# One pool of PSUM banks, a first tile in four units, and small decay groups in a fused scan and two-product kernel

## The chip, the cores and the metric

The kernel runs on one core of a Trainium2 chip. The metric is the time of one execution on the device in microseconds (us), the median of several runs. The core has five engines with queues of their own: TensorE (PE; its weight loads are PEld), VectorE (DVE), ScalarE (ACT), GpSimd (POOL) and SyncE (SP), which here issues all transfers.

## The reference

The first half is a gated linear recurrence over 768 steps, for 4 batches of 8 heads of 48 elements. The second is two matrix products with a function between them, on 3072 tokens of 384 elements.

```python
f = 1 / (1 + exp(-f_logit))                       # gate per step, head and key element
state = f[t, :, None] * state + k[t] (outer) v[t] # 48 x 48 per batch and head
y[t] = q[t] @ state
x = y as (4*768 tokens, 8*48)
h = x @ w_in                                      # 384 -> 2048
out = (h * cos(h)) @ w_out                        # 2048 -> 384, float32
```

## The kernel before

**Attention.** The 768 steps of each batch are cut into six chunks of 128 steps, 24 chunks in all. Four loads bring a chunk (`chunk_load`, line 254: f, k, q, v, each 192 KB). `decay_group` (lines 259 to 296) takes three chunks at a time: exponential and logarithm of the gates on ScalarE (lines 267, 270), a cumulative sum over the steps on TensorE with a triangular matrix (line 280), and two exponentials of it, b and bi (line 290). `attend` (lines 298 to 435) scales q and k with them on GpSimd (qtd and ktd, lines 301 and 304), copies v among zeros (vz, line 307), transposes q and k on TensorE (line 318), copies the transposes out (qdt and kz, lines 332 and 334), forms the scores (pa, line 349), masks them (am, line 354), updates the state (ps, st, sz, lines 369 to 388) and sums the output (py, lines 416 and 420) into the tile xT of 512 tokens (lines 432 and 434).

**The two products.** `moe` (lines 438 to 473) works on a tile of 512 tokens, six tiles in all. For each of 16 blocks of 128 hidden features it makes three matmuls into one bank (ph, line 445), a sine on ScalarE (cos(h) as sin(h + pi/2), line 448) and a product on VectorE (gT, line 451). Then for each 128 tokens 16 matmuls form the result (po, line 459), which is copied (line 467) and stored (line 472).

**The order.** Nothing is left to a scheduler at run time. The class `Plan` takes each operation with the engines that may do it and a cost in ns for each, plans them one by one, and the kernel issues them in the order of planned start times. `Plan.run` (lines 77 to 145) chooses, among the operations whose inputs have been planned, the one with the smallest key: planned start, then the priority value (smaller first). An operation that would change ScalarE's function table has 1300 added to the start in its key (lines 109 to 111). The exponential and logarithm share one table (E), the sine has another (S). When the first E operation of a decay group is placed, ScalarE takes no operation with a table from outside the group until all of the group's are placed (the lock, lines 107 and 125). Attention's priority is its chunk's number, that of the products 1000 plus the tile's number (line 493).

**Buffers.** Each kind of tile has its own slots, and a slot is held from the first planned writer to the last planned user. The eight PSUM banks are split: three for ph, one for po, two for pa, two for everything else of attention (lines 217 to 220). Weights are loaded through two staging tiles each for w_in and w_out and cast by VectorE (line 242); the loads are planned behind chunks 1, 2 and 3. Tiles that must be zero outside the written parts are filled at the start, vz, kz and sz on GpSimd (lines 204 to 209).

Of the kernel before, what the change touches and what calls it, by code (L numbers as in the profile page):

```python
# [15 lines left out]
class Slots:  # L16


    def __init__(self, aps):
        self.aps = aps  # L20
        self.free_at = [0.0] * len(aps)
        self.held = [False] * len(aps)

    def best(self):
        free = [(t, i) for i, t in enumerate(self.free_at) if not self.held[i]]
        return min(free) if free else None


class Val:


    def __init__(self, pool=None, ap=None):
        self.pool, self._ap, self.slot = pool, ap, None
        self.writers, self.uses = [], 0

    @property
    def ap(self):
        return self._ap if self.pool is None else self.pool.aps[self.slot]

# [6 lines left out]
class Plan:  # L46
# [7 lines left out]
    def op(self, eng, fn, reads=(), writes=(), prio=0.0, table=None, lat=0.0, grp=None):  # L54
# [6 lines left out]
        for v in writes:  # L61
            if not v.writers and v.pool is not None:
                o.alloc.append(v)
            elif v.writers:

                o.deps.add(v.writers[-1])
        for v in list(reads) + list(writes):
            if v.pool is not None and v not in o.vals:
                o.vals.append(v)
                v.uses += 1  # L70
# [6 lines left out]
    def run(self):  # L77
# [13 lines left out]
        while len(order) < n:  # L91
            best = None
            for o in ready:
# [3 lines left out]
                for v in o.alloc:  # L97
                    b = v.pool.best()
                    if b is None:
                        ok = False  # L100
                        break
                    at = max(at, b[0] + self.SEM)
                if not ok:
                    continue
                for e, cost in o.eng.items():
                    s = max(at, free[e])
                    if e == "ACT" and lock is not None and o.grp != lock and o.table is not None:
                        continue
                    k = s
                    if e == "ACT" and o.table is not None and o.table != table:  # L110
# [4 lines left out]
                    if best is None or key < best[0]:  # L115
                        best = (key, s, o, e, cost)
            assert best is not None, "no op can be placed"
# [8 lines left out]
            for v in o.alloc:  # L126
                _, i = v.pool.best()
                v.slot = i
                v.pool.held[i] = True
# [3 lines left out]
            for v in o.vals:  # L133
                v.uses -= 1
                v.pool.free_at[v.slot] = max(v.pool.free_at[v.slot], o.end)
                if not v.uses:
                    v.pool.held[v.slot] = False
# [11 lines left out]
def kernel(  # L149
# [21 lines left out]
    GRP = 3  # L171
# [9 lines left out]
    def slots(name, n, shape, dt=BF16, zero=None):  # L181
# [6 lines left out]
        return Slots(aps)  # L188

    def banks(name, n):  # L190
        return Slots([ppool.tile([128, 512], F32, name=f"{name}_{i}") for i in range(n)])

    nld = 4
# [17 lines left out]
    xS = slots("xT", NT, [128, KM, TOK])  # L211
    gS = slots("gT", 2, [128, KF, TOK])
    coS = slots("cosh", 4, [128, TOK])
    otS = slots("ot", 4, [128, d_model], F32)
    wiS = slots("wi32", 2, [128, KM, 512], F32)
    woS = slots("wo32", 2, [128, 4, d_model], F32)
    phS = banks("ph", 3)
    poS = banks("po", 1)
    paS = banks("pa", 2)
    miS = banks("mi", 2)  # L220
# [4 lines left out]
    N128 = 62.0  # L225
# [6 lines left out]
    def load_weights(part, i, prio):  # L232
        if part == 0:
            st, dst = Val(wiS), w_in_v[i]
            src = moe_w_in.rearrange("(km p) f -> p km f", p=128)[:, :, i * 512:(i + 1) * 512]
        else:
            st, dst = Val(woS), w_out_v[i]
            src = moe_w_out.rearrange("(kf p) m -> p kf m", p=128)[:, i * 4:(i + 1) * 4, :]
        P.op({"SP": 2000.0}, lambda e, st=st, src=src: nc.sync.dma_start(out=st.ap, in_=src),
             writes=[st], prio=prio, lat=2200.0)  # L240
        P.op({"DVE": 900.0},
             lambda e, st=st, dst=dst: nc.vector.tensor_copy(out=dst.ap, in_=st.ap),
# [3 lines left out]
    xT = [Val(xS) for _ in range(NT)]  # L246
# [12 lines left out]
    def decay_group(chunks, g, prio):  # L259

        outs = []
        for (b, c, ld) in chunks:
# [9 lines left out]
            e1 = P.op({"ACT": 500.0}, act1, reads=[f], writes=[f], prio=prio, table="E", grp=g)  # L272
            P.op({"ACT": 500.0}, act2, reads=[f], writes=[sp], prio=prio, table="E", grp=g)
            outs.append((b, c, ld, sp))
        res = []
        for (b, c, ld, sp) in outs:
# [15 lines left out]
            P.op({"ACT": 470.0}, ex, reads=[pc], writes=[bt], prio=prio, table="E", grp=g)  # L292
            P.op({"ACT": 470.0}, lambda e, pc=pc, bi=bi, ex=ex: ex(e, pc, bi, 1.0, H * D),
# [4 lines left out]
    def attend(b, c, ld, bt, bi, prio):  # L298
        _, kf, qf, vf = ld
        qtd, ktd, vz = Val(qtdS), Val(ktdS), Val(vzS)  # L300
        P.op({"POOL": 1000.0}, lambda e: nc.gpsimd.tensor_mul(  # L301
            out=qtd.ap[:, :, 0:D], in0=qf.ap,
            in1=bt.ap[:, 0:H * D].rearrange("p (h d) -> p h d", d=D)), reads=[qf, bt], writes=[qtd], prio=prio)
        P.op({"POOL": 1000.0}, lambda e: nc.gpsimd.tensor_mul(  # L304
            out=ktd.ap[:, :, 0:D], in0=kf.ap,
            in1=bi.ap.rearrange("p (h d) -> p h d", d=D)), reads=[kf, bi], writes=[ktd], prio=prio)
        P.op({"POOL": 620.0}, lambda e: nc.gpsimd.tensor_copy(
# [28 lines left out]
        both = {"DVE": 420.0, "ACT": 600.0}  # L336
# [88 lines left out]
        x = xT[tok // TOK]  # L425
        off = tok % TOK

        def yev(e):
            d = x.ap[:, :, off:off + C]
# [5 lines left out]
        P.op({"ACT": 480.0, "DVE": 540.0}, yev, reads=[py], writes=[x], prio=prio)  # L435


    def moe(t, prio):
        x, gT = xT[t], Val(gS)
        for j in range(KF):  # L440
            ph, co = Val(phS), Val(coS)

            def g1(e, j=j, ph=ph):
                for m in range(KM):
                    nc.tensor.matmul(ph.ap, lhsT=w_in_bf[:, m, j * 128:(j + 1) * 128],  # L445
                                     rhs=x.ap[:, m, :], start=(m == 0), stop=(m == KM - 1))
            P.op({"PE": 3 * 216.0}, g1, reads=[x, w_in_v[j // 4]], writes=[ph], prio=prio, lat=170.0)
            P.op({"ACT": 600.0}, lambda e, ph=ph, co=co: nc.scalar.activation(  # L448
                out=co.ap, in_=ph.ap, func=AF.Sin, bias=halfpi),
                reads=[ph], writes=[co], prio=prio, table="S")  # L450
            P.op({"DVE": 665.0}, lambda e, j=j, ph=ph, co=co: nc.vector.tensor_mul(  # L451
                out=gT.ap[:, j, :], in0=ph.ap, in1=co.ap),
                reads=[ph, co], writes=[gT], prio=prio)
        for i in range(TOK // 128):
# [15 lines left out]
            P.op({"ACT": 480.0, "DVE": 540.0}, ev, reads=[po], writes=[ot], prio=prio)  # L470
            r0 = t * TOK + i * 128
            P.op({"SP": 500.0}, lambda e, ot=ot, r0=r0: nc.sync.dma_start(
                out=out[r0:r0 + 128, :], in_=ot.ap), reads=[ot], prio=prio, lat=2000.0)
# [5 lines left out]
    wjobs = [(0, i) for i in range(NW)] + [(1, i) for i in range(KF // 4)]  # L479
    done = 0  # L480
    for g in range(len(chunks) // GRP):
        grp = []
        for j, (b, c) in enumerate(chunks[g * GRP:(g + 1) * GRP]):
            n = g * GRP + j
            grp.append((b, c, chunk_load(b, c, float(n))))
            if n >= 1 and wjobs:
                for w in wjobs[:3]:
                    load_weights(*w, prio=n + 0.5)
                wjobs = wjobs[3:]
        for j, item in enumerate(decay_group(grp, g, float(g * GRP))):  # L490
# [44 lines left out]
```

## Time and profile before

| | |
|---|---|
| median of 3 runs | 274.25 us (273.5 to 277.42) |
| profiled execution, its own time | 276.98 us |
| its span, first to last instruction | 274.9 us |
| mean granted clock of TensorE | 0.944 |
| bytes moved | 25.17 MB read, 4.72 MB written |

The span is what the profile's rows cover; the execution's own time has 2.1 us around it. In the rows a line as L445 is a line of the kernel, "a<-b" is output and inputs by the program's names, "x16" a count, and square brackets give the idle time before and what ended it. "mi" is the name of attention's shared banks, "PEclk" the clock granted to TensorE as a part of 2.4 GHz, and SPq is the queue of SyncE.

### The profile page before, as it was taken

Reading aid. Unit: us, or ns where it says so; the run is one execution under the profiler, and the core shown is the slowest. Engines: PE = TensorE matmul, PEld = TensorE weight load, DVE = VectorE, ACT = ScalarE, POOL = GpSimd, SP = SyncE. Lnnn points to the kernel's source line nnn. Section 1 sums busy time; section 2 is a strip of 40 time slices with the busy share of each in tenths; the row PEclk is TensorE's granted clock in tenths of the full one; section 3 lists DMA queues with packets and bytes.
Section 4 is the critical chain, followed back from the end, with each engine's and each line's share of the span. In section 5 each row is a group of like instructions: output and inputs, shape, how many; then the busy total and the mean of one; then the engine's idle time right before and its main releaser. Section 6 shows DMA issues by size and latency. Waiting matters only on the chain.

```text
span 274.9 us, 4372 instructions
## 1 busy us (share of the span) xinstructions
PE 210.6 (77%) x1603; PEld 134.9 (49%) x1616; DVE 138.0 (50%) x234; ACT 147.7 (54%) x268; POOL 87.0 (32%) x122
## 2 busy tenths in 40 slices
PE   0056627767658668665888999999999999999984
PEld 0046415456547557554753554554454454455442
DVE  4037825445654545774688435525534633823700
ACT  4224225566684664657678457546646645753711
POOL 9964233747696556858600000000000000000000
PEclk9999999977997757999599999999999999999999
DMA  7944999999999999970000010010011011010011
GB/s 149 294 100 136 343 241 261 209 184 211 180 211 193 219 216 190 202 143 4 0 1 2 29 57 29 31 53 32 8 52 58 0 60 57 0 58 30 29 58 57
DMA packets 107028, 30.15 MB, mean 110 GB/s; under 512 B 100352, under 2 KB 105472, under 8 KB 107008
## 3 DMA queue, kind: packets, MB, share of 16 engines
q1 hardware_dynamic: 107008, 29.89, 46.1%
q8 instruction: 12, 0.20, 0.3%
q14 instruction: 8, 0.07, 0.1%
HBM read 25.17 MB, written 4.72 MB: 109 GB/s over the span
## 4 chain that ended last, share of the span: by engine, by line
PE 56%; DVE 15%; ACT 13%; POOL 6%; issue 5%; DMA 3%; SPq 1%; DVEq 0%; POOLq 0%; ACTq 0%
PE po L459 23%; PE ph L445 16%; PE mi L416 6%; DVE gT L451 5%; ACT cosh L448 4%; DVE am L354 4%; PE mi L318 4%; PE pa L349 4%; DMA f<-in_f_logit_dram 3%; ACT kz L332 3%; DVE kz L334 3%; PE mi L420 2%; ACT qdt L332 2%; POOL vz L186 2%; DVE qdt L334 1%
## 5 line engine op out<-in xcount | busy, mean ns | idle before, releaser
L451 DVE TENSOR_TENSOR gT<-ph,cosh 128x512 bf16<-128x512 f32 x96 | 63.8, 691 | 57.3 <-ACT cosh L448 57.3
L445 PE MATMUL ph<-xT,w_in_bf 128*128 128x512 bf16 x275 | 68.5, 380 | 5.2 <-DVE gT L451 4.2
L448 ACT ACTIVATE cosh<-ph,halfpi 128x512 bf16<-128x512 f32 x96 | 63.5, 687 | 10.3 <-PE ph L445 10.3
L459 PE MATMUL po<-w_out_bf,gT 128*128 128x384 bf16 x384 | 66.3, 326 | 1.7 <-ACT ot L467 1.7
L459 PEld LDWEIGHTS <-gT 128*128 128x128 bf16 x384 | 37.5, 98 | 29.3 <-issue 2.4
L445 PEld LDWEIGHTS <-w_in_bf 128*128 128x128 bf16 x288 | 28.0, 97 | 38.9 <-issue 10.1
L416 PE MATMUL mi<-am,vz 128*128 128x128 bf16 x240 | 28.4, 252 | 15.7 <-DVE kz L334 5.5
L467 ACT COPY ot<-po 128x384 f32<-128x384 f32 x24 | 11.5, 479 | 48.7 <-PE po L459 48.7
L354 DVE TENSOR_TENSOR am<-pa,umask 128x512 bf16<-128x512 f32 x48 | 31.0, 685 | 11.9 <-PE pa L349 11.8
L301 POOL TENSOR_TENSOR qtd<-q,b 128x384 bf16<-128x384 f32 x24 | 24.0, 999 | 30.7 <-ACT b L290 22.6
L349 PE MATMUL pa<-qdt,kz 128*128 128x128 bf16 x192 | 21.4, 257 | 11.3 <-ACT kz L332 8.6
L416 PEld LDWEIGHTS <-vz 128*128 128x128 bf16 x240 | 20.5, 114 | 18.6 <-issue 11.9
L304 POOL TENSOR_TENSOR ktd<-k,bi 128x384 bf16<-128x384 f32 x24 | 23.9, 998 | 0.1
L349 PEld LDWEIGHTS <-kz 128*128 128x128 bf16 x192 | 15.0, 115 | 15.1 <-ACT kz L332 11.0
L280 PE MATMUL mi<-sp,umask 128*128 128x384 bf16 x24 | 9.7, 405 | 16.5 <-ACT sp L270 12.5
L388 POOL TENSOR_TENSOR sz<-st,b 64x192 bf16<-64x192 f32 x32 | 16.7, 523 | 16.8 <-DVE st L380 13.6
L334 DVE COPY qdt<-mi 128x512 bf16<-128x512 bf16 x11 | 4.7, 424 | 33.6 <-PE mi L318 31.9
L332 ACT COPY kz<-mi 64x512 bf16<-64x512 bf16 x20 | 11.6, 580 | 17.5 <-DVE qdt L334 15.9
L420 PE MATMUL mi<-qdt,sz 128*128 128x128 bf16 x120 | 19.6, 253 | 0.0
L318 PE MATMUL mi<-ident,qtd 128*128 128x128 bf16 x96 | 12.1, 264 | 8.3 <-POOL qtd L301 7.3
L267 ACT ACTIVATE f<-f 128x384 f32<-128x384 f32 x24 | 12.6, 526 | 9.4 <-DMA f<-in_f_logit_dram 9.3
L432 ACT CAST xT<-mi 128x384 bf16<-128x384 f32 x17 | 8.1, 479 | 16.6 <-PE mi L420 14.1
(37 smaller groups left out, 183.0 us busy)
## 6 DMA issues: line engine op xcount, KB each, us to landing
f<-in_f_logit_dram SPq DMA_DIRECT2D x24, 192.0 KB, 3.7
k<-in_k_dram SPq DMA_DIRECT2D x24, 192.0 KB, 3.7
q<-in_q_dram SPq DMA_DIRECT2D x24, 192.0 KB, 3.9
v<-in_v_dram SPq DMA_DIRECT2D x24, 192.0 KB, 3.8
out_dram<-ot SPq DMA_DIRECT2D x24, 192.0 KB, 1.8
wi<-in_moe_w_in_dram SPq DMA_DIRECT2D x4, 768.0 KB, 6.7
wo<-in_moe_w_out_dram SPq DMA_DIRECT2D x4, 768.0 KB, 7.8
```

Source lines behind the costliest of these rows:

```text
L301: P.op({"POOL": 1000.0}, lambda e: nc.gpsimd.tensor_mul(out=qtd.ap[:, :, 0:D], in0=qf.ap, in1=bt.ap[:, 0:H * D].rearrange("p (h d) -> p h ...
L304: P.op({"POOL": 1000.0}, lambda e: nc.gpsimd.tensor_mul(out=ktd.ap[:, :, 0:D], in0=kf.ap, in1=bi.ap.rearrange("p (h d) -> p h d", d=D)), r ...
L318: nc.tensor.transpose(out=o[:, j + p, :], in_=t.ap[:, 2 * p:2 * p + 2, :].rearrange("p h d -> p (h d)"), identity=ident)
L332: nc.scalar.copy(out=d, in_=s)
L349: nc.tensor.matmul(o[:, i, :], lhsT=kz.ap[:, h // 2, h % 2, :], rhs=qdt.ap[:, h // 2, :], start=(i == 0), stop=(i == 3))
L354: nc.vector.tensor_mul(out=am.ap, in0=pa.ap.rearrange("p (a n) -> p a n", n=C), in1=umask[:, None, :].broadcast_to([128, 4, C]))
L416: nc.tensor.matmul(o[:, t, :], lhsT=vz.ap[:, w0:w0 + 128], rhs=ams[n // 4].ap[:, n % 4, :], **fl)
L420: nc.tensor.matmul(o[:, t, :], lhsT=S_in.ap[:, n, w0:w0 + 128], rhs=qdt.ap[:, n, :], **fl)
L445: nc.tensor.matmul(ph.ap, lhsT=w_in_bf[:, m, j * 128:(j + 1) * 128], rhs=x.ap[:, m, :], start=(m == 0), stop=(m == KM - 1))
L448: P.op({"ACT": 600.0}, lambda e, ph=ph, co=co: nc.scalar.activation(out=co.ap, in_=ph.ap, func=AF.Sin, bias=halfpi), reads=[ph], writes=[c ...
L451: P.op({"DVE": 665.0}, lambda e, j=j, ph=ph, co=co: nc.vector.tensor_mul(out=gT.ap[:, j, :], in0=ph.ap, in1=co.ap), reads=[ph, co], writes ...
L459: nc.tensor.matmul(po.ap[:, 0:d_model], lhsT=gT.ap[:, j, i * 128:(i + 1) * 128], rhs=w_out_bf[:, j, :], start=(j == 0), stop=(j == KF - 1))
```

## The change

- **PSUM.** All eight banks are one pool. Each kind has a cap on how many it holds at a time: ph 4, po 2, pa 2, the rest of attention 4, and ph and po together 5.
- **The first 512 tokens** go through both products in four units of 128 tokens. In such a unit one bank takes four blocks of hidden features side by side, 12 matmuls of 128 columns; gT of a unit has slots of its own (gc). Tokens 512 to 3071 stay in tiles of 512.
- **Readiness.** xT is tracked in pieces of 128 tokens, and gT in parts, so that a matmul of the second product waits only for the parts that it reads.
- **Decay groups** are 1, 1, 1, 1, 2 and then six times 3 chunks, and the first exponential of a group waits for the gates (f) of all its chunks.
- **Planner.** The operation's engine is the one where it ends first, a table switch of 1300 ns counted in; the key is then its start without the switch, and the priority. The products' priority is no longer 1000 and more but two chunks behind the attention of their own first token (LEAD), rising through the unit.
- **Engines.** qtd and ktd may go to VectorE or GpSimd; weight casts to VectorE, ScalarE or GpSimd; the zero fills of vz, kz and sz go from GpSimd to VectorE. Several planned costs are changed.
- **Loads.** Five buffers in place of four; weights share three staging tiles; w_in is planned right behind chunk 0, w_out from chunk 1 to chunk 3.

The diff, without the helpers' renamed bookkeeping:

```diff
+class Banks:
+    def __init__(self, base, name, cap, groups=()):
+        self.base, self.name, self.caps = base, name, [[cap, 0]] + list(groups)
+    def best(self):
+        return self.base.best() if all(n < cap for cap, n in self.caps) else None
+    def take(self, i):
+        self.base.held[i] = True
+        for c in self.caps:
+            c[1] += 1
...
+class Part:
+    def __init__(self, whole, cut):
+        self.whole, self.cut, self.writers = whole, cut, []
...
+                pick = None
                 for e, cost in o.eng.items():
-                    s = max(at, free[e])
                     if e == "ACT" and lock is not None and o.grp != lock and o.table is not None:
                         continue
-                    k = s
-                    if e == "ACT" and o.table is not None and o.table != table:
-                        k = s + 1300.0
-                    key = (k + (cost if len(o.eng) > 1 else 0.0), o.prio, o.seq)
-                    if len(o.eng) > 1:
-                        key = (k, o.prio, o.seq, cost)
...
+                    s = max(at, free[e])
+                    sw = 1300.0 if e == "ACT" and o.table not in (None, table) else 0.0
+                    if pick is None or s + cost + sw < pick[0]:
+                        pick = (s + cost + sw, s, e, cost)
+                if pick is None:
+                    continue
+                key = (pick[1], o.prio, o.seq)
...
-    GRP = 3
+    GROUPS = [1, 1, 1, 1, 2] + [3] * 6
+    LEAD = 2.0
...
-    nld = 4
+    nld = 5
-    vzS = slots("vz", 4, [128, H * VW + 128], zero=nc.gpsimd)
+    vzS = slots("vz", 4, [128, H * VW + 128], zero=nc.vector)
-    kzS = slots("kz", 3, [128, NP, 2, C], zero=nc.gpsimd)
+    kzS = slots("kz", 3, [128, NP, 2, C], zero=nc.vector)
-    szS = slots("sz", 3, [128, NP, SW], zero=nc.gpsimd)
+    szS = slots("sz", 3, [128, NP, SW], zero=nc.vector)
...
-    phS = banks("ph", 3)
-    poS = banks("po", 1)
-    paS = banks("pa", 2)
-    miS = banks("mi", 2)
+    base = banks("ps", 8)
+    moe_cap = [5, 0]
+    phS = Banks(base, "ph", 4, [moe_cap])
+    poS = Banks(base, "po", 2, [moe_cap])
+    paS = Banks(base, "pa", 2)
+    miS = Banks(base, "mi", 4)
-    N128 = 62.0
+    N128 = 56.0
...
-        P.op({"DVE": 900.0},
-             lambda e, st=st, dst=dst: nc.vector.tensor_copy(out=dst.ap, in_=st.ap),
+        P.op({"DVE": 1700.0 if part == 0 else 950.0, "ACT": 1450.0, "POOL": 2400.0}, cast,
              reads=[st], writes=[dst], prio=prio)
...
+            for (_, _, ld2) in chunks:
+                e1.deps.add(ld2[0].writers[0])
...
-        P.op({"POOL": 1000.0}, lambda e: nc.gpsimd.tensor_mul(
+        P.op({"POOL": 1000.0, "DVE": 560.0}, lambda e: E(e).tensor_mul(
             out=qtd.ap[:, :, 0:D], in0=qf.ap,
...
-    def moe(t, prio):
-        x, gT = xT[t], Val(gS)
-        for j in range(KF):
+    def moe(t0, T):
+        n0 = t0 // C
+        xs, gT = xT[n0:(t0 + T) // C], Val(gS if T == TOK else gcS)
+        x = x_sb[t0 // TOK][:, :, t0 % TOK:t0 % TOK + T]
+        G = 512 // T
+        span = T / C
+        for j in range(KF // G):
...
+                for g in range(G):
+                    f0 = (j * G + g) * 128
+                    for m in range(KM):
+                        nc.tensor.matmul(ph.ap[:, g * T:(g + 1) * T],
+                                         lhsT=w_in_bf[:, m, f0:f0 + 128], rhs=x[:, m, :],
+                                         start=(g == 0 and m == 0),
+                                         stop=(g == G - 1 and m == KM - 1))
+            pr = LEAD + n0 + 0.5 * span * j * G / KF
...
+            pr = LEAD + n0 + 0.5 * span + 0.5 * i
...
-                P.op({"PE": 4 * 163.0}, g2, reads=[gT, w_out_v[s]], writes=[po], prio=prio,
-                     lat=170.0 if s == 3 else 0.0)
+                P.op({"PE": 4 * 162.5}, g2,
+                     reads=[gT.parts[q] for q in range(4 * s // G, (4 * s + 3) // G + 1)] + [w_out_v[s]],
+                     writes=[po], prio=pr, lat=170.0 if s == 3 else 0.0)
...
+    for i in range(NW):
+        load_weights(0, i, 0.2 + 0.1 * i)
+    for i in range(KF // 4):
+        load_weights(1, i, 1.2 + 0.5 * i)
+    units = [C] * (TOK // C) + [TOK] * (NT - 1)
```

## Rows read from the trace of the kernel before

**Rows 1.** The page's busy time of each engine over the span.
```profile
PE 210.6 (77%) x1603; PEld 134.9 (49%) x1616; DVE 138.0 (50%) x234; ACT 147.7 (54%) x268; POOL 87.0 (32%) x122
```

**Rows 2.** Two stretches: start and end, length, busy us per engine, clock, DMA share, GB/s.
```profile
core 0: us, PE busy (x) PEld busy (x) DVE busy (x) ACT busy (x) POOL busy (x), PEclk, DMA share, GB/s
60.00:140.00 80.00, 55.63 (x678) 47.22 (x678) 46.84 (x91) 51.06 (x106) 52.83 (x75) 0.82 0.80 157
140.00:272.00 132.00, 125.87 (x672) 65.33 (x680) 63.28 (x96) 73.37 (x118) 0.00 (x0) 1.00 0.10 35
```

**Rows 3.** The first product's matmuls alone (line 445), 16 to 139 us: PE, PEld.
```profile
16.00:139.00 123.00, 2.43 (x8) 1.10 (x10) 0.88 0.82 177
```

**Rows 4.** The chain of waits, both products after 140 us: start, us, what.
```profile
151.48 2.60 PE po L459 x16
...
154.08 1.29 PE ph L445 x6
...
173.34 2.60 PE po L459 x16
```

**Rows 5.** Timeline of TensorE, attention of a chunk: start, us, engine, line, operation, count.
```profile
87.23 0.33 PE L416 MATMUL mi<-am,vz 128*128 128x128 bf16 x3 [1.15 <-ACT bi L290]
...
88.12 0.61 PE L349 MATMUL pa<-qdt,kz 128*128 128x128 bf16 x8
88.57 0.33 PE L369 MATMUL mi<-vz,ktd 128*128 128x96 bf16 x4
88.85 0.39 PE L318 MATMUL mi<-ident,qtd 128*128 128x128 bf16 x4
...
91.15 0.34 PE L280 MATMUL mi<-sp,umask 128*128 128x384 bf16 x1 [1.69 <-DVE sz L388]
```

**Rows 6.** The same timeline, an early stretch with the same operation.
```profile
22.59 1.06 PE L349 MATMUL pa<-qdt,kz 128*128 128x128 bf16 x8
```

**Rows 7.** SP's queue: loads of f of the sixth and the last chunk, 18 chunks apart.
```profile
45.12 0.65 SPq L254 DMA_DIRECT2D f<-in_f_logit_dram  x1
...
115.78 0.65 SPq L254 DMA_DIRECT2D f<-in_f_logit_dram  x1
```

**Rows 8.** A stretch of weight loads, as in rows 2.
```profile
30.00:35.00 5.00, 3.08 (x24) 2.58 (x25) 4.71 (x6) 0.70 (x2) 1.01 (x2) 1.00 1.03 350
```

**Rows 9.** ScalarE's timeline: chunk 3 from its first exponential to its rows in xT.
```profile
36.60 0.52 ACT L267 ACTIVATE f<-f 128x384 f32<-128x384 f32 x1 [2.20 <-DMA f<-in_f_logit_dram]
...
46.56 0.48 ACT L432 CAST xT<-mi 128x384 bf16<-128x384 f32 x1 [0.34 <-PE mi L420]
```

**Rows 10.** ScalarE's timeline around the one table switch.
```profile
132.52 0.59 ACT L332 COPY qdt<-mi 128x512 bf16<-128x512 bf16 x1 [0.43 <-PE mi L318]
133.13 1.28 ACT L448 ACT_TABLE_LOAD   x1
134.42 1.84 ACT L448 ACTIVATE cosh<-ph,halfpi 128x512 bf16<-128x512 f32 x3
```

**Rows 11.** Groups by shape: ScalarE's logarithm and exponential; busy us, mean ns, idle before.
```profile
L270 ACT ACTIVATE sp<-f 128x384 bf16<-128x384 f32 x24 | 12.5, 522 | 0.7
L290 ACT ACTIVATE b<-mi 128x388 f32<-128x388 f32 x24 | 11.9, 495 | 8.7 <-PE mi L283 7.2 <-POOL ktd L304 0.7 <-POOL vz L307 0.6
```

**Rows 12.** The chain at the start, zero fills and the first product on GpSimd.
```profile
1.70 4.93 POOL vz L186 x4
...
13.76 0.96 POOL qtd L301
```

**Rows 13.** VectorE's timeline, first zero fills.
```profile
0.86 1.37 DVE L186 MEMSET sp<- 128x256 uint32 x5 [0.86 <-PEq L519]
```

**Rows 14.** Waits: who for whom, us in total, times, longest.
```profile
SPq L239 <- DVE w_in_bf L242: 8.2, 2, 7.6
...
ACT f L267 <- DMA f<-in_f_logit_dram: 9.3, 6, 2.2
```

**Rows 15.** The end: the last copy of a result.
```profile
271.73 0.48 ACT L467 COPY ot<-po 128x384 f32<-128x384 f32 x1 [2.85 <-PE po L459]
```

More of the change, by code (lines that the diff above doesn't have):

```diff
@@ L26, in best, with aps, take, used @@
         return min(free) if free else None
+class Banks:
+    def __init__(self, base, name, cap, groups=()):
+        self.base, self.name, self.caps = base, name, [[cap, 0]] + list(groups)
+    @property
+    def aps(self):
+        return self.base.aps
+    def best(self):
+        return self.base.best() if all(n < cap for cap, n in self.caps) else None
+    def take(self, i):
+        self.base.held[i] = True
+        for c in self.caps:
+            c[1] += 1
+    def used(self, i, t):
+        self.base.free_at[i] = max(self.base.free_at[i], t)
+    def drop(self, i):
+        self.base.held[i] = False
+        for c in self.caps:
+            c[1] -= 1
 class Val:
@@ L97, in run @@
                 for v in o.alloc:
+                    if v.slot is not None:
+                        continue
                     b = v.pool.best()
@@ L126, in run @@
             for v in o.alloc:
+                if v.slot is not None:
+                    continue
                 _, i = v.pool.best()
                 v.slot = i
-                v.pool.held[i] = True
+                v.pool.take(i)
             o.start, o.end = s, s + cost + o.lat
@@ L187, in slots @@
             aps.append(t)
-        return Slots(aps)
+        return Slots(aps, name)
     def banks(name, n):
-        return Slots([ppool.tile([128, 512], F32, name=f"{name}_{i}") for i in range(n)])
-    nld = 4
+        return Slots([ppool.tile([128, 512], F32, name=f"{name}_{i}") for i in range(n)], name)
+    nld = 5
     fS = slots("f", nld, [128, H, D], F32)
@@ new lines, in moe @@
+            pr = LEAD + n0 + 0.5 * span * j * G / KF
+            P.op({"PE": G * 3 * (T / 2.4 + 2.0)}, g1, reads=xs + [w_in_v[j * G // 4]],
+                 writes=[ph], prio=pr, lat=170.0)
+            P.op({"ACT": 640.0}, lambda e, ph=ph, co=co: nc.scalar.activation(
+                out=co.ap, in_=ph.ap, func=AF.Sin, bias=halfpi),
+                reads=[ph], writes=[co], prio=pr, table="S")
+            gv = gT.part(lambda a, j=j: a[:, j * G:(j + 1) * G, 0:T])
+            P.op({"DVE": 650.0}, lambda e, ph=ph, co=co, gv=gv: nc.vector.tensor_mul(
+                out=gv.ap, in0=ph.ap.rearrange("p (g t) -> p g t", t=T),
+                in1=co.ap.rearrange("p (g t) -> p g t", t=T)),
+                reads=[ph, co], writes=[gv], prio=pr)
@@ L455, in moe @@
+        for i in range(T // 128):
             po, ot = Val(poS), Val(otS)
+            pr = LEAD + n0 + 0.5 * span + 0.5 * i
             for s in range(4):
@@ L478 @@
     chunks = [(b, c) for b in range(B) for c in range(NCH)]
-    wjobs = [(0, i) for i in range(NW)] + [(1, i) for i in range(KF // 4)]
-    done = 0
-    for g in range(len(chunks) // GRP):
-        grp = []
[L483 to L490, printed above, removed]
-            attend(*item, prio=float(g * GRP + j))
-        while done < NT and (done + 1) * TOK <= (g + 1) * GRP * C:
-            moe(done, prio=1000.0 + done)
-            done += 1
+    for i in range(NW):
[3 more added lines that the diff above has]
+    units = [C] * (TOK // C) + [TOK] * (NT - 1)
+    n, t0 = 0, 0
+    for g, size in enumerate(GROUPS):
+        grp = []
+        for j, (b, c) in enumerate(chunks[n:n + size]):
+            grp.append((b, c, chunk_load(b, c, float(n + j))))
+        for j, item in enumerate(decay_group(grp, g, float(n))):
+            attend(*item, prio=float(n + j))
+        n += size
+        while units and t0 + units[0] <= n * C:
+            moe(t0, units[0])
+            t0 += units.pop(0)
     order = P.run()
```

101 lines of the change are left out of this document (58 added, 43 removed).

## The prediction

> **What bounds the kernel now.** I read the engines' totals first. TensorE is the busiest at 210.6 of 274.9 us, and ScalarE and VectorE stand at 147.7 and 138.0 [rows 1]. No engine is full, so the two halves have to be read apart. In the windows, 140 to 272 us is full: TensorE is busy 125.9 of 132 us at a granted clock of 1.00. From 60 to 140 us it is busy only 55.6 of 80 us, at 0.82, and no other engine is busier [rows 2]. What TensorE does in the first half says why. Between 16 and 139 us it issues 8 matmuls of the first product, of 288 in all [rows 3]. The 24 chunks of attention come first, and then nearly all of both products. The order is the planner's: it charges a sine that changes ScalarE's table 1300 ns in the key by which it chooses, so sines yield to the exponentials as long as there are any.
>
> The chain of waits gives the second half's price: one token tile starts 21.86 us after another (151.48 to 173.34), and six tiles are 131 us [rows 4]. Inside a tile 16 matmuls of the second product take 2.60 us and 6 of the first 1.29 us. A tile has 64 and 48 of them: 10.4 + 10.3 = 20.7 us without a gap.
>
> The first half is set by loads. The gates' loads of 18 successive chunks are issued in 70.7 us, 3.93 us a chunk [rows 7], with the DMA engines full in the weight loads too, at 350 GB/s [rows 8]; a weight block of 786 KB takes 2.25 us by that, eight 18 us. All loads together are 24 x 3.93 + 18 = 112 us. So DMA could end long before TensorE's work does, and the products could fill TensorE's gaps. That is what this change would have to get.
>
> **TensorE's work.** A chunk's attention at the 2.4 GHz level: the output's 16 matmuls go from 87.23 to 88.12 (0.89 us), eight for the scores 0.45, four for the state 0.28, eight transposes at the scores' pace 0.45, the cumulative sum 0.34 [rows 5]. That is 2.41 us. All the work is 24 x 2.41 + 6 x 20.7 = 182 us. The new ScalarE total is 147.7 plus some 20 table loads, about 174; VectorE has 138.0 plus 7 of zero fills plus those products that it takes over from GpSimd. Both stay below 182 plus TensorE's idle start, so TensorE becomes the bound, with less slack on ScalarE than before.
>
> **The sum, part by part.**
> *Start, 65 us until full tiles are ready.* Tile 1 (chunks 4 to 7) needs chunk 7, whose group is 6 to 8 and now waits for the gate of chunk 8. Before that gate DMA moves eight chunks and eight weight blocks, 31.4 + 18 us, plus its own quarter chunk and 1 us of launch: about 52. From a gate to the rows of xT a chunk took 36.60 to 47.04, 10.4 us [rows 9]. The two other gates' exponential and logarithm go first, four at 0.52 [rows 11], 2.1 us. So about 65. The weights now stand ahead of chunks 1 to 3 in SP's queue; that is counted here. Ends: 60 if the chain is shorter at the higher clock; 73 if a weight block waits for its staging tile as now, 8.2 us in SP's queue [rows 14], with the later chunks queued behind it.
>
> In these 65 us TensorE has nine chunks and tile 0 in 128-token units to do, 9 x 2.41 + 20.7 = 42 us, in the some 50 us after chunk 0. That only just fits, since early matmuls run at the lower level: eight took 1.06 us at 22.59, against 0.61 later [rows 6, 5]. I take 3 us over; ends 0, and 17 if half of this work is left at 65.
>
> *After that*, 15 chunks x 2.41 = 36.2 and 5 tiles x 20.7 = 103.5. With four banks for the first product in place of three, I take the tile without its gaps; the other end is today's 21.86, +6.
>
> *Table switches.* Five groups of three lie in this stretch. Each takes ScalarE away from the sine for two loads and twelve activations: 2 x 1.28 [rows 10] + 6 x 0.52 + 6 x 0.49 [rows 11] = 8.6 us. TensorE has work that needs no sine: per three chunks 7.2 us of attention and 7.8 of the second product, 15 in a period of 22.8. Spread evenly, 8.6 x 15/22.8 = 5.7 us of each lock is covered, and 2.9 lies open: 5 x 2.9 = 15. Ends: 0 if the planner puts the second product into the locks, 43 if they are all open.
>
> The price of one switch is 1.30 us: the copy before the load ends at 133.11, and the sine starts at 134.42 [rows 10]. The Trainium skill (ScalarE: Activation LUTs, What ACT_TABLE_LOAD costs) gives 1283 ns for the load, which the row agrees with, and 1380 ns for a drain, which the row does not show. By the page the ten switches would cost 13.8 us more, and the sum would be 241.
>
> *The end.* The last tile has nobody else's work to fill its gaps: 21.86 - 20.7, 1.2 us. From the last copy's start to the span's end are 274.9 - 271.7 = 3.2 [rows 15].
>
> *Edits at or near nothing.* The zero fills leave GpSimd, where they hold the first product back to 13.76 us [rows 12], for VectorE, where 256 words take 0.27 us [rows 13]: 6720 words, 7.1 us, done at about 11. Gain for chunk 0 is between 2.7 and 8 us, but tile 1 waits for gates, so it counts nothing; without that cover it would be those 2.7 to 8. The group's wait for its gates stands ahead of everything later in ScalarE's queue, sines too. Loads run faster than they are needed from tile 1 on (3.93 against 7.6 us of TensorE's work a chunk), so it costs nothing there; the wait for gates today is 9.3 us [rows 14], and that is the end above. Result stores now stand between loads in SP's queue, which stops at each until its copy is done; five buffers of loads cover it, and a stop longer than some four chunks of TensorE's work would starve it. Weight casts and products that may go to another engine move work between engines with room.
>
> Sum: 65 + 3 + 36.2 + 103.5 + 15 + 1.2 + 3.2 = 227 us of span. The profiled execution took 276.98 with a span of 274.9, 2.1 more, and 2.7 above the median of 274.25. So 227 + 2.1 - 2.7 is about **227**.
>
> **Rivals.**
> *TensorE stays full* (0.16). All locks are covered and the start leaves nothing over: 65 + 139.7 + 3.2 = 208 of span, 207. For it: after 140 us three banks already keep the gaps at 1.2 us a tile [rows 4]. Against it: an order fixed in advance on four engines, with three of them at three quarters of their time.
>
> *The locks lie open* (0.16). TensorE has used up attention and second product when a lock comes, since both also go ahead whenever a bank is free. Then the 43 replaces the 15: 255. The Trainium skill (ScalarE: Activation LUTs, Rules for kernel authors) speaks for it: do all of one table set before switching, which is what the old order does. In the rows one switch alone is to be seen, and it bears out neither.
>
> *The clock falls* (0.04), slower than before. Interleaving leaves small gaps everywhere where 140 to 272 us had none. At 0.82 granted from 60 to 140 us [rows 2], 36% of that time was at 1.2 GHz, with TensorE busy 70%. If the share s of the 139.7 us of work runs at half speed, the time is 227 + 139.7 s; above s = 0.38 that is over 280. Against it: work at the lower level fills the gaps that caused it, and 95% busy had 1.00. The Trainium skill (TensorE: Matmul & The Clock Gate, HAM oscillation) tells of bursts between waits falling back to the half clock each time; 60 to 140 us agrees, the second half has none.
>
> *The order doesn't change* (0.05). Exponentials have the lower priority value and could still all go before the sines; then only the start is gained, 274 - 7 = 267. Against it: the key now leaves the switch out, and a sine may start as soon as ScalarE has nothing earlier.
>
> **Chances and range.** Forecast 0.59 (own range 214 to 242), rivals as given. The range takes in the full TensorE and nearly all of the open locks: 206 to 254. I leave out the upper part of the open locks, the last two rivals and small tails. The runs of before lie within 1.4%, so 2% is what can be told from no change: below 268.8 faster, above 279.7 slower. Forecast, both middle rivals and half of the last are faster: 0.92; same 0.04; slower 0.04.
>
> **What would show it.** After: sines and logarithms side by side from about 20 us on; ScalarE with some 20 table loads of 1.28 us, each followed at once by its activation; tile pitch near 21 us plus attention; TensorE at 80% or more from 65 us to the end at a clock near 1.00; gates' loads still 3.9 us apart while buffers last, then slower. The prediction is wrong if TensorE waits over 20 us for sines or their products, if SP's queue stands behind stores while TensorE idles, or if tile 1 starts after 75 us.

## The result and the profile after

The changed kernel takes 230.16 us (median of 4 runs, 228.87 to 230.77) against 275.29 us for the kernel before on the same chip: a ratio of 0.835, 95% interval 0.828 to 0.843. The forecast was 227 us, with a range from 206 to 254. The profiled execution took 229.88 us with a span of 228.1. A run over 1.5% above the fastest of its own kernel counts as disturbed and is left out of the ratios below: three of the four with one table (228.84 to 230.13 us), and one each with attention at two banks (233.93) and with the products at three banks and one (232.91).

The page's first part, to be set against [rows 1]:

```profile
PE 195.5 (86%) x1751; PEld 130.5 (57%) x1760; DVE 156.0 (68%) x274; ACT 165.8 (73%) x286; POOL 47.7 (21%) x78
```

TensorE is the bound, as forecast, and ScalarE and VectorE stand at about 70%. GpSimd has lost nearly half its work: of the 24 scalings of q and of k each, 17 now run on VectorE, and so do the zero fills.

The windows of the changed kernel, from tile 1's first matmul to tile 5's and from there to the end, against [rows 2] (columns as there):

```profile
core 0: us, PE busy (x) PEld busy (x) DVE busy (x) ACT busy (x) POOL busy (x), PEclk, DMA share, GB/s
73.30:204.00 130.70, 121.59 (x1035) 77.20 (x1041) 92.00 (x154) 97.99 (x179) 33.66 (x49) 0.97 0.46 102
204.00:228.00 24.00, 20.84 (x111) 10.84 (x111) 10.34 (x16) 12.26 (x20) 0.00 (x0) 1.00 0.09 33
```

In the first, attention of fifteen chunks and four tiles run side by side, and TensorE is busy 121.6 of 130.7 us. Before, 60 to 140 us had 55.6 of 80. The second is the last tile alone. In the chain of waits it reads as follows, to be set against [rows 4] and [rows 15]:

```profile
204.41 10.09 PE ps L525 x46
214.50 10.41 PE ps L546 x64
224.94 0.48 ACT ot L555
```

With the copy's start at 224.94, tile 5 has run from 203.98 in 21.0 us. The two products follow each other without a wait. Before, with three banks, every third block of the first product waited for the bank that a sine and a product on VectorE had just given back:

```profile
165.76 0.66 PE ph L445 x3
166.45 0.70 ACT cosh L448
167.17 0.70 DVE gT L451
167.91 0.82 PE ph L445 x3
```

ScalarE's timeline shows the interleaving, and it carries one answer to [rows 10] and one to [rows 9]:

```profile
59.20 0.48 ACT L505 CAST xT<-ps 128x384 bf16<-128x384 f32 x1
59.70 1.28 ACT L590 ACT_TABLE_LOAD   x1
61.00 0.94 ACT L338 ACTIVATE f<-f 128x384 f32<-128x384 f32 x2
...
72.50 0.48 ACT L505 CAST xT<-ps 128x384 bf16<-128x384 f32 x1 [1.05 <-PE ps L494]
```

The first exponential starts within 0.02 us of the load's end, so a switch costs its 1.28 us and nothing behind it. There are 16 loads in all, not some 20. From this group's first exponential to the last rows of tile 1 (chunk 7's, copied at 72.50) are 61.00 to 72.98, 12.0 us, where the sum had 10.4 + 2.1. Tile 1's first matmul starts at 73.28.

SP's queue shows when the gates of this group, chunks 6 to 8, were asked for (against [rows 7]; the column after the start is how long the issue took):

```profile
35.92 0.93 SPq L325 DMA_DIRECT2D k<-in_k_dram  x1
40.65 0.36 SPq L560 DMA_DIRECT2D out_dram<-ot  x1
41.05 0.76 SPq L325 DMA_DIRECT2D q<-in_q_dram  x1
...
45.61 1.18 SPq L325 DMA_DIRECT2D f<-in_f_logit_dram  x1
48.73 0.36 SPq L560 DMA_DIRECT2D out_dram<-ot  x1
...
56.27 0.65 SPq L325 DMA_DIRECT2D f<-in_f_logit_dram  x1
```

The line at 56.27 issues the gate of chunk 8, which landed 3.4 us later, at 59.7. That is also when ScalarE ended the copy that stands ahead of the group (59.20 + 0.48), so its queue was not idle for the gate. Twice a result store stands in the queue before its copy is done, and the loads behind it stand too. The waits of that queue before 58 us name it: 3.7 us for ScalarE's copy and 1.9 us for VectorE's.

### The profile page after: what moved, and what is told of

Its sections match the earlier page's. It is cut to its first block, busy times and chain, and to the rows that moved or that the text cites. A ratio compares the mean times of both kernels' runs of the same rounds, so it can differ in the third digit from the quotient of the medians.

```text
span 228.1 us, 4657 instructions
## 1 busy us (share of the span) xinstructions
PE 195.5 (86%) x1751; PEld 130.5 (57%) x1760; DVE 156.0 (68%) x274; ACT 165.8 (73%) x286; POOL 47.7 (21%) x78
## 4 chain that ended last, share of the span: by engine, by line
PE 66%; DVE 15%; ACT 12%; issue 5%; POOL 0%; DVEq 0%; ACTq 0%
PE ps L525 27%; PE ps L546 26%; PE ps L490 5%; ACT kz L406 3%; PE ps L423 3%; DVE am L428 3%; PE ps L392 2%; ACT bi L363 2%; PE ps L494 2%; ACT b L363 2%; ACT L532 2%; DVE qtd L375 1%; DVE ktd L378 1%; DVE gc L536 1%; DVE kz L408 1%
## 5 line engine op out<-in xcount | busy, mean ns | idle before, releaser
L525 PE MATMUL ps<-xT,w_in_bf 128*128 128x512 bf16 (+1 forms) x423 | 68.6, 320 | 3.1 <-DVE gT L536 0.9
L532 ACT ACTIVATE cosh<-ps,halfpi 128x512 bf16<-128x512 f32 x96 | 60.9, 692 | 5.0 <-PE ps L525 3.1
L546 PE MATMUL ps<-w_out_bf,gT 128*128 128x384 bf16 x320 | 53.6, 326 | 0.0
L536 DVE TENSOR_TENSOR gT<-ps,cosh 128x512 bf16<-128x512 f32 x80 | 50.5, 686 | 4.2 <-ACT cosh L532 4.1
L428 DVE TENSOR_TENSOR am<-ps,umask 128x512 bf16<-128x512 f32 x48 | 30.6, 684 | 26.0 <-PE ps L423 25.3
L490 PE MATMUL ps<-am,vz 128*128 128x128 bf16 x240 | 23.2, 226 | 1.0 <-DVE am L428 1.0
L423 PE MATMUL ps<-qdt,kz 128*128 128x128 bf16 x192 | 18.1, 231 | 5.5 <-ACT kz L406 3.2
L494 PE MATMUL ps<-qdt,sz 128*128 128x128 bf16 x120 | 16.9, 224 | 0.0
L406 ACT COPY kz<-ps 64x512 bf16<-64x512 bf16 x26 | 15.1, 580 | 2.1 <-DVE kz L408 1.3
L546 PE MATMUL ps<-w_out_bf,gc 128*128 128x384 bf16 x64 | 13.6, 349 | 1.4 <-DVE gc L536 0.7
```

The lines of the kernel that those rows point to most:

```text
L406: nc.scalar.copy(out=d, in_=s)
L423: nc.tensor.matmul(o[:, i, :], lhsT=kz.ap[:, h // 2, h % 2, :], rhs=qdt.ap[:, h // 2, :], start=(i == 0), stop=(i == 3))
L428: nc.vector.tensor_mul(out=am.ap, in0=pa.ap.rearrange("p (a n) -> p a n", n=C), in1=umask[:, None, :].broadcast_to([128, 4, C]))
L490: nc.tensor.matmul(o[:, t, :], lhsT=vz.ap[:, w0:w0 + 128], rhs=ams[n // 4].ap[:, n % 4, :], **fl)
L494: nc.tensor.matmul(o[:, t, :], lhsT=S_in.ap[:, n, w0:w0 + 128], rhs=qdt.ap[:, n, :], **fl)
L525: nc.tensor.matmul(ph.ap[:, g * T:(g + 1) * T], lhsT=w_in_bf[:, m, f0:f0 + 128], rhs=x[:, m, :], start=(g == 0 and m == 0), stop=(g == G - ...
```

## The experiments

Each was timed in three rounds beside the kernel before; ratios are to it, with 95% intervals. Three questions were asked: which part carries the gain, what the banks do, and whether the terms of the sum are what they were called.

**The order alone.** The kernel before with the planner's key and the priority changed.

```diff
-                        k = s + 1300.0
+                        k = s
...
-            moe(done, prio=1000.0 + done)
+            moe(done, prio=2.0 + 4.0 * done)
```

> The kernel before with one thing changed: the planner's key leaves the table switch out, and the products' priority is 2 plus the tile's first chunk in place of 1000 and more. Banks, groups, tile size, loads and zero fills stay as before. Theory (the gain is that sines may stand between exponentials, so that the products fill TensorE's gaps): at least two thirds of the 45 us come by this alone, 245 us or less. Rival (the shared banks or the 128-token units are what lets the halves overlap): 258 us or more. Second rival (without the other parts the switches cost what the overlap brings): 270 to 280.

It took 263.26 us, ratio 0.956 (0.949 to 0.962). The theory falls: the order by itself brings 13 of the 45 us. The halves do overlap, but TensorE waits on the way, and in the mixed stretch it is busy 75% (waits of TensorE, then the window; waits are in all, times, longest):

```profile
PE ph L445 <- DVE gT L451: 5.4, 12, 1.4
PE mi L416 <- DVE st L380: 5.3, 5, 1.4
PE mi L416 <- ACT bi L290: 4.0, 5, 1.0
PE mi L318 <- DVE st L380: 2.6, 3, 0.9
```
```profile
50.00:155.00 105.00, 78.26 (x871) 56.91 (x877) 66.11 (x125) 86.21 (x156) 58.98 (x84) 0.97 0.72 146
```

The output's matmuls (L416) do not read st or bi, nor do the transposes (L318) read st. What they wait for, by the code, is the bank that those operations read last.

**The old split of banks** in the changed kernel.

```diff
-    base = banks("ps", 8)
-    moe_cap = [5, 0]
-    phS = Banks(base, "ph", 4, [moe_cap])
-    poS = Banks(base, "po", 2, [moe_cap])
-    paS = Banks(base, "pa", 2)
-    miS = Banks(base, "mi", 4)
+    phS = banks("ph", 3)
+    poS = banks("po", 1)
+    paS = banks("pa", 2)
+    miS = banks("mi", 2)
```

> The changed kernel with the banks divided as before: three for the first product, one for the second, two and two for attention. Theory (the order of the work is the gain, and banks give the 1.2 us of gaps per tile and some waits in the mixed stretch): 234 to 242 us. Rival (attention and products overlap only because banks are shared): 250 or more. Second rival (banks give nothing): 228 to 232.

254.2 us, ratio 0.922 (0.916 to 0.927): 24 us of the 45 are gone, and the time lies in the rival's range. The waits of TensorE are of the same kind:

```profile
PE mi L390 <- DVE st L452: 5.7, 4, 2.0
PE mi L488 <- DVE st L452: 4.7, 4, 1.4
...
PE mi L488 <- DVE kz L406: 3.4, 2, 2.0
PE mi L441 <- DVE xT L505: 2.4, 2, 1.4
PE mi L488 <- ACT bi L361: 2.4, 4, 0.7
```

None of these is a wait for an operand: transposes (L390) wait for the state's sum (st), the output (L488) for that, for the copies of the transposes and for an exponential, the state (L441) for the rows of xT. With the rest of the kind (another 3 to 4 us) they make some 22 us at attention's two banks. The products' own banks add 4.2 us (2.2 for ph, 2.0 for po).

**Which banks?** One side at a time at its old number, from the shared pool.

```diff
-    miS = Banks(base, "mi", 4)
+    miS = Banks(base, "mi", 2)
```

> The changed kernel with attention's general cap at two banks in place of four; the products keep four and two of at most five. With the old split of banks it took 254.2 us, 24 more, and TensorE waited there for the copies that empty attention's two banks. Theory A (those two banks are nearly the whole of the 24 us, since sum, transposes, state and output of a chunk go through them one after another): 244 to 256 us. Theory B (the products' three and one banks are it, since they run dry in ScalarE's locks): 229 to 234 us.

```diff
-    phS = Banks(base, "ph", 4, [moe_cap])
-    poS = Banks(base, "po", 2, [moe_cap])
+    phS = Banks(base, "ph", 3, [moe_cap])
+    poS = Banks(base, "po", 1, [moe_cap])
```

> The changed kernel with the products at three banks and one, as before, and attention at four and two. Theory A (attention's two banks were the cost of the old split): 229 to 235 us. Theory B (the products' banks): 244 to 256 us. If both this and attention at two banks lie near 240, the two costs add.

231.32 us, ratio 0.835 (0.827 to 0.843), and 230.05 us, ratio 0.830 (0.822 to 0.839). Neither costs anything that can be told from the changed kernel, so neither side's number alone is the cause: 24 us are lost by the split, and 0 by either half of its numbers.

**The old numbers from one pool.** Both edits together, so that every kind may hold what it held in the split.

> The changed kernel with one pool of eight banks, but with every cap as the old split had it: three and one for the products, two and two for attention. Each side alone at its old caps cost 1 us or nothing, while the old split took 254.2 us. Theory C (not the number but the choice counts: from a pool the planner takes the bank that has been free longest, so a copy later than planned holds nobody up, while in a split of one to three banks the next user follows at once): 229 to 234 us. Theory D (the two halves' limits only bite together): 246 to 256 us.

234.37 us, ratio 0.846 (0.842 to 0.850), some 3 to 4 us over the changed kernel and 20 under the split. Theory C holds for 20 of the 24 us. What is left of the waits for a bank:

```profile
PE ps L525 <- DVE am L428: 0.8, 1, 0.8
...
PE ps L423 <- DVE st L454: 0.3, 1, 0.3
...
PE ps L392 <- ACT bi L363: 0.2, 1, 0.2
```

They sum to 1.3 us (1.5 with 0.2 for gT) in place of some 22 and the products' 4, and the span is 252.2 - 232.7 = 19.5 us shorter. In the stretch from 60 to 140 us TensorE is busy 69.2 us with the pool and 58.5 with the split (the split first):

```profile
60.00:140.00 80.00, 58.49 (x658) 43.92 (x661) 59.94 (x106) 69.82 (x127) 26.46 (x39) 0.94 0.79 158
```
```profile
60.00:140.00 80.00, 69.23 (x700) 47.64 (x703) 59.57 (x110) 68.11 (x129) 31.18 (x44) 0.96 0.81 166
```

The code says how. The planner counts a bank as given back when the last operation on it has been planned, though that operation ends later. In a split the next user of the kind must take that same bank and wait; from the pool it takes another that has been free for long. The runs do not tell apart whether the loss is in the planned order, which is made with those waits in it, or in copies that come later than planned.

**Order and banks, all else undone.**

```diff
-    GROUPS = [1, 1, 1, 1, 2] + [3] * 6
+    GROUPS = [3] * 8
-    nld = 5
+    nld = 4
-    units = [C] * (TOK // C) + [TOK] * (NT - 1)
+    units = [TOK] * NT
-            for (_, _, ld2) in chunks:
-                e1.deps.add(ld2[0].writers[0])
-        P.op({"POOL": 1000.0, "DVE": 560.0}, lambda e: E(e).tensor_mul(
+        P.op({"POOL": 1000.0}, lambda e: E(e).tensor_mul(
...
```

> The changed kernel with everything undone but the planner's key and priorities, the parts of xT and gT, and the shared banks: first tile of 512, eight groups of three without the wait for gates, four load buffers, zero fills on GpSimd, products of attention on GpSimd only, weights cast by VectorE and loaded behind chunks 1 to 3. Theory (order and banks are the gain, the start is worth some 5 us by the 128-token units and little by the rest): 235 to 242 us. Rival (the other parts carry more than that together): 245 to 255. With the key alone it was 263.3.

241.65 us, ratio 0.873 (0.870 to 0.877), at the upper edge of what the theory gave. Of the gain of 45 us, 35 come with the order and the pool together, against 13 for the order alone; all other parts bring about 10 more. The 22 us between the two fit the 24 that the split costs. (The tracking by parts, the rule by which an engine is picked, the shared staging tiles and the changed planned costs stay in it.) The pool without the new order was not run.

**The first tile in one piece.**

```diff
-    units = [C] * (TOK // C) + [TOK] * (NT - 1)
+    units = [TOK] * NT
```

> The changed kernel with the first 512 tokens as one tile again. Theory (units of 128 tokens let the first tile's work fill the start, where TensorE has nothing else; the rest of the time TensorE is full): tile 0 can then begin only with chunk 3, near 43 us, so about 5.2 us of work for each of the two to three units that ran before that is moved behind: 238 to 246 us. Rival (there is idle time enough between 43 and 73 us, before tile 1 is ready, to take the whole tile): 228 to 233.

235.45 us, ratio 0.853 (0.847 to 0.859): 5.3 us more, between theory and rival. From 20 to 60 us TensorE is busy 34.9 us in the changed kernel and 27.1 without units (the changed kernel first):

```profile
20.00:40.00 20.00, 15.60 (x162) 11.98 (x161) 12.68 (x23) 15.01 (x21) 4.84 (x7) 0.83 0.94 253
40.00:60.00 20.00, 19.32 (x261) 15.72 (x259) 16.31 (x32) 19.01 (x34) 3.94 (x8) 1.00 0.87 180
```
```profile
20.00:40.00 20.00, 10.89 (x89) 8.42 (x89) 12.05 (x19) 7.34 (x15) 4.48 (x7) 1.00 0.98 262
40.00:60.00 20.00, 16.23 (x104) 9.24 (x105) 10.96 (x21) 12.97 (x24) 5.13 (x9) 1.00 1.10 216
```

In the first window the changed kernel's clock is 0.83 against 1.00, so part of its busy time there is slower matmuls: 15.6 x 0.83 is some 13 us of full-speed work, an estimate. Without units TensorE gets part of the difference back, since from 60 to 80 us it is busy 18.2 us at a clock of 1.00 against 15.9 at 0.91. Another thing shows in this trace: no store stands in SP's queue before 66.75 us, and the gate of chunk 8 is issued at 50.29, 6 us earlier than in the changed kernel.

**The wait for the gates.**

```diff
-            for (_, _, ld2) in chunks:
-                e1.deps.add(ld2[0].writers[0])
```

> The changed kernel without the wait of a group's first exponential for the gates of all its chunks. The prediction's start (68 us until tile 1) had about 4 us from this wait, two more chunks' loads at 3.93 us less what a lock then stands open. Theory (the wait costs the start and gives nothing later, since loads run ahead): 226 to 229 us. Rival (without it the lock stands open while ScalarE waits for a gate, and sines wait behind): 233 to 240. Third: same within 1 us, since in the plan the loads are early enough either way.

228.8 us, ratio 0.828 (0.822 to 0.834): the interval holds the changed kernel's ratio, so no difference is shown. Tile 1 starts at 74.45 us in its trace, not earlier than the 73.28 of the changed kernel. So the theory's reason, an earlier start, did not happen.

**One table.**

```diff
-                out=co.ap, in_=ph.ap, func=AF.Sin, bias=halfpi),
+                out=co.ap, in_=ph.ap, func=AF.Exp, bias=halfpi),
...
-                if o.table == "E" and table != "E":
+                if table is None:
```

> The changed kernel with the sine's place taken by an exponential of the same shape with the same bias, so that the cosine is not computed, and the table loaded once. The planner's order stays word for word; the 15 later table loads of 1.28 us are gone. Theory (a third of a lock is open, as in the prediction's sum): 19 us of ScalarE are worth 4 to 8 us, so 222 to 226. Rival (every load stands in TensorE's way): 211 to 213. Second rival (all hidden, TensorE is the bound throughout): 229 to 231.

One of the four runs took 225.22 us, 5 less than the changed kernel; the three others (228.84, 229.82, 230.13) save 0 to 1.3 us. What is excluded is the rival of 211 to 213: ScalarE has 19.2 us less to do, and TensorE, the bound, hardly gains. The page of the run of 228.84 us, to be set against the first fence:

```profile
PE 194.0 (85%) x1751; PEld 129.2 (57%) x1760; DVE 156.4 (69%) x274; ACT 146.6 (65%) x271; POOL 47.6 (21%) x78
```

Between the theory of 4 to 8 us and the one that hides everything these runs do not decide. Only the loads are gone in them: the planner's locks and their activations stand where they stood.

**More lead for attention.**

```diff
-    LEAD = 2.0
+    LEAD = 4.0
```

> The changed kernel with the products' priority four chunks behind attention in place of two. In its trace the last three chunks are finished only after tile 4: TensorE waits 195 to 204 us in the attention of chunks 21 to 23, some 2 to 3 us idle and 10 us in all in which VectorE and ScalarE are empty. Theory (attention taken earlier fills tile 4's gaps, and tile 5 follows tile 4 at once): 225 to 228 us. Rival (TensorE's work is the same, and what it does not do there it does elsewhere): 229 to 231. Second rival (attention ahead holds banks that the products need): 232 to 240.

233.94 us, ratio 0.846 (0.840 to 0.853): some 3 to 4 us slower, so the theory falls. It does fill the gap that it was made for, and pays earlier (lead 2 first, then lead 4):

```profile
145.00:185.00 40.00, 39.11 (x303) 23.41 (x306) 31.71 (x54) 34.98 (x62) 9.13 (x13) 1.00 0.11 31
185.00:205.00 20.00, 18.01 (x168) 12.35 (x167) 7.58 (x14) 7.55 (x16) 2.01 (x4) 1.00 0.11 40
```
```profile
145.00:185.00 40.00, 35.79 (x318) 22.59 (x316) 27.18 (x47) 28.03 (x50) 8.77 (x13) 0.96 0.11 31
185.00:205.00 20.00, 19.48 (x145) 11.72 (x146) 13.06 (x23) 14.06 (x26) 1.94 (x4) 1.00 0.06 21
```

TensorE's idle time goes from 2.0 to 0.5 us in the second window and from 0.9 to 4.2 in the first, and the clock is no longer full there. The time lies in the second rival's range, but its reason does not show in the first window. Of TensorE's 3.8 us of waits there 0.6 are for a bank, and none is a wait of the products; the longest, 2.1 us, is the scores' wait for their operand kz:

```profile
PE ps L423 <- DVE kz L408: 2.1, 1, 2.1
PE ps L392 <- DVE st L454: 0.6, 1, 0.6
```

**The zero fills back on GpSimd.**

```diff
-    vzS = slots("vz", 4, [128, H * VW + 128], zero=nc.vector)
+    vzS = slots("vz", 4, [128, H * VW + 128], zero=nc.gpsimd)
...
```

(kz and sz likewise.)

> The changed kernel with the zero fills of vz, kz and sz back on GpSimd. The prediction priced the move at nothing, since tile 1 waits for gates, with 2.7 to 8 us for chunk 0. Theory (hidden): within 2 us of 230. Rival (TensorE is short of work only at the start, so what unit 0 loses is never made up): 233 to 238 us, TensorE's first unit some 3 to 8 us later in the trace and all that follows too.

229.54 us, ratio 0.829 (0.825 to 0.834): no difference. The first unit starts at 18.45 us here and at 17.39 in the changed kernel, and tile 1 at 72.78 and 73.28: the 1.1 us are made up by then.

**Scaling on GpSimd only**, and no wait for gates.

```diff
-        P.op({"POOL": 1000.0, "DVE": 560.0}, lambda e: E(e).tensor_mul(
+        P.op({"POOL": 1000.0}, lambda e: E(e).tensor_mul(
```

> The changed kernel without the wait for gates (228.8 us alone) and with the scaling of q and k on GpSimd only, as before. In the changed kernel GpSimd is busy 21% and 17 of 24 scalings of each kind run on VectorE at 718 and 775 ns, against 560 planned. Theory (VectorE's overrun delays the copies and masks that TensorE waits for): 225 to 228 us. Rival (GpSimd's 1000 ns each lengthen every chunk's chain and the end of attention): 230 to 235. Third: within 1 us of 228.8.

229.69 us, ratio 0.830 (0.826 to 0.833): the third case, 0.9 us off the run without the wait alone and inside its interval. VectorE has 135.7 us to do in place of 152.2, and that changes nothing.

No version beat the changed kernel by more than can be told: the lowest median is 228.8.

## Why the prediction was right, and where it was not

*What bounds the kernel* was read rightly. TensorE, with 182 us of work by the sum and 195.5 us busy by the page, became the bound: from tile 1's first matmul to the end it is busy 142.4 of 154.8 us. The second half's idle engines were what the change filled.

*The start* was 73.3 us, not 68. The chain from the first exponential to tile 1's rows came out (12.0 us for 12.5), so the miss lies ahead of it. Chunk 8's gate was to land at about 52 us and landed at 59.7, and the table load of 1.28 us behind it was not in this part of the sum. In the prediction's text the step that failed is "five buffers of loads cover it", said of the stores in SP's queue. The loads did not run ahead yet at 35 to 50 us, and two stops of 3.7 and 1.9 us held them; without units, where no store stands ahead of it, the same gate is issued 6 us earlier. That these stops are what moved tile 1 is not shown. ScalarE was busy 19.0 and TensorE 19.3 of the 20 us from 40 to 60, so an earlier gate alone would have found both at work. In the run with the products at three banks and one, this gate is issued at 53.78, 2.5 us earlier, and tile 1 starts at 74.59. Without the wait for gates it is issued at 55.10, and tile 1 starts at 74.45. The other candidate is TensorE's work in the start, for which the text had 42 us: from its first unit to tile 1 (17.39 to 73.28) TensorE is busy 48.6 us, at a mean clock of 0.91. Between the two the cause of the 5.3 us stays open. The zero fills did hide (chunk 0 lost 1.1 us by them, where the text had 2.7 to 8), and so did the wait for gates.

*After that*, 130.7 us to tile 5's start, where the sum had 15 x 2.41 + 4 x 20.7 + 15 = 134. TensorE is busy 121.6 us of them, for 119 in the sum, and idles 9.1. So the 15 us that the sum put down to locks cover all idle time and more. The waits of TensorE in this stretch say that locks are hardly in it:

```profile
PE ps L423 <- ACT kz L406: 1.7, 4, 0.6
PE ps L392 <- DVE qtd L375: 1.6, 3, 0.7
PE ps L392 <- DVE ktd L378: 1.5, 3, 0.9
PE ps L392 <- DVE st L454: 1.2, 1, 1.2
PE ps L525 <- DVE gT L536: 0.9, 1, 0.9
```

Only the last, 0.9 us, stands behind a sine; the others are attention's own operands and a bank. (Whether ScalarE's copies of kz came late because of a lock was not separated.) The sum's term for the locks was thus much too large, and attention's own waits and 2.6 us more of work, which it did not have, came in its place. That the number nearly holds is luck in this part.

*The end* was 24.1 us from tile 5's start (203.98 to 228.1), against 20.7 + 1.2 + 3.2 = 25.1.

So 227 and a span of 228.1 agree by +5.3 - 3.3 - 1.0: misses that nearly cancel. The agreement to a microsecond is luck, not insight. Two small figures of the text do not come out either, and neither moves the forecast: half of 42 us of work is 21, not 17, and the chances named for a faster kernel add up to 0.935, not 0.92.

*The banks* are the term that was mis-sized without hurting the number. The text gave them 1.2 us a tile, 6 us as the bound. It reckoned the mixed stretch from TensorE's work, as if a bank were always to be had, and that is true of the pool only: with the old split TensorE waits some 22 us for attention's banks, and the time is 254. The prediction saw the old split cost little in [rows 4], where one kind of work ran. It did not ask what the split costs when two kinds run at once.

*The rivals.* The locks did not lie open: TensorE waited 0.9 us behind a sine, not 43. The clock fell in places (0.78 from 65 to 85 us, 0.97 over the mixed stretch), far from the 38% at which it would have decided. The order did change.

The Trainium skill (ScalarE: Activation LUTs, Rules for kernel authors) says to do all of one table set before the other. The order before keeps that rule, and the changed one breaks it with 16 loads where there were 2. Here, without 15 of the loads, the time is 0 to 5 us shorter in four runs, and the order and the pool that go with the loads bring 35. The drain of 1380 ns that the Trainium skill (ScalarE: Activation LUTs, What ACT_TABLE_LOAD costs) counts with each load does not show in this trace: a copy ended at 59.68, the load stood from 59.70 to 60.98, and the exponential started at 61.00.

## What to carry to other kernels

When two halves of a kernel use different engines, ask of each resource that they share what it does when both run, not what it costs one of them alone: the same eight banks cost 1.2 us a tile in one half and 24 us in the mix. In an order planned beforehand, a pool from which the longest free buffer is taken can be worth more than the number of buffers of each kind; here the pool gave 20 us, and the larger numbers 3 to 4 at most. And a queue that issues both loads and stores passes a late store's wait on to the loads (3.7 and 1.9 us here); before calling that the cause of a late start, look at whether the engines behind the loads were idle. Here they were not.

## What the runs showed of the hardware that was not expected

A product on VectorE with both operands in SBUF (128x384, float32 in, bfloat16 out) took 718 and 775 ns on average, while an addition of the same shape with one operand in PSUM took 546 ns. The means hide two cases. The 14 products up to 64.4 us, while GpSimd had nothing to do, took 0.55 to 0.56 us each. The other 20, nearly all beside work on GpSimd, took 0.88 us on average (worked out from the two means). The two groups, then one product of each case and two of GpSimd's:

```profile
L375 DVE TENSOR_TENSOR qtd<-q,b 128x384 bf16<-128x384 f32 x17 | 12.1, 718 | 14.5 <-ACT b L363 14.5
L454 DVE TENSOR_TENSOR st<-ps,sz 128x384 f32<-128x384 f32 x16 | 8.7, 546 | 0.1
```
```profile
64.37 0.56 DVE L378 TENSOR_TENSOR ktd<-k,bi 128x384 bf16<-128x384 f32 x1 [0.23 <-ACT bi L363]
119.59 1.35 DVE L378 TENSOR_TENSOR ktd<-k,bi 128x384 bf16<-128x384 f32 x1
```
```profile
119.33 1.19 POOL L375 TENSOR_TENSOR qtd<-q,b 128x384 bf16<-128x384 f32 x1
120.48 1.31 POOL L378 TENSOR_TENSOR ktd<-k,bi 128x384 bf16<-128x384 f32 x1
```

GpSimd's own products took 1115 and 1191 ns on average in the changed kernel, and 999 and 998 both before and in the run with scaling on GpSimd only, where VectorE has none of them. So VectorE's products with both operands in SBUF and GpSimd's work took longer when they ran side by side, and the planned 560 and 1000 ns are too short there. In the last experiment, taking these products off VectorE gained nothing.
